# Weighted sums over 32 keys for two query blocks at once, in a fused sparse-attention and feed-forward kernel on one core

## The chip, the cores and the metric

The kernel runs on one core of a Trainium2 chip. The core has a matrix engine (TensorE, "PE" in the profile, with its weight loads shown apart as "PEld"), a vector engine (VectorE, "DVE"), a scalar engine (ScalarE, "ACT"), GpSimd ("POOL") and SyncE ("SP"), whose queue issues nearly all transfers here. Each engine works through its own list of instructions in order and waits on semaphores for the others. The metric is the device time of one execution in microseconds (us); less is better. Before the change it is 864.33 us, the median of 3 runs (864.06 to 865.29).

## The reference

Eight batches of eight heads, 576 positions, head size 64: four heads attend to a local band, four to a strided pattern; then a feed-forward layer over all 4608 tokens with a softplus between its two matrix products.

```python
rel = pos[:, None] - pos[None, :]
mask_local = (rel >= 0) & (rel < stride)                       # stride = 32
mask_strided = (rel >= 0) & (pos[None, :] % stride == pos[:, None] % stride)
scores = np.where(masks, q @ k.T / sqrt(64), -1e9)             # local for heads 0-3, strided for 4-7
attn = softmax(scores)                                         # with 1e-9 added to the sum
x = (attn @ v) laid out as (batch * position, head * 64)       # 4608 x 512
h = x @ w_in                                                   # 512 -> 2048
g = np.maximum(h, 0.0) + np.log1p(np.exp(-np.abs(h)))
out = g @ w_out                                                # 2048 -> 512
```

## The kernel before

**Pairs and chunks.** Heads are worked off in pairs, four pairs a batch, 32 pairs in all, numbered n = 0 to 31 in the order of work. The strided heads' positions are sorted by class on the host, so that for both kinds a block of 32 queries needs only its own block of 32 keys and the block ahead of it: 64 keys. A pair has 18 such query blocks; they are laid out as 9 "chunks" (x = 0 to 8) times two "places" (place 0: the first nine blocks of a head, place 1: the last nine). From the third batch on (n = 8 and up) this is the layout of `head_scores`, `add_mask`, `turn` and `late_sums`, which the change touches; the first eight pairs use other routines.

**One pair, from n = 8 on.** All of its matrix work is in fp32, and each matmul of the program runs as two passes on TensorE, each with a weight load: the trace counts two MATMUL and two LDWEIGHTS for each.

- `head_scores` (L406 to L428, all its matmuls at L422, task S): for each chunk, place and head a matmul with 64 rows of contraction (the head's dimensions), 32 queries as the weights and 64 keys as the moving operand: 36 matmuls. A tile of the array is set by the rows that a matmul reads (64 for each head) and by the partitions that it writes (32 for each query block). Chunks 0 to 5 ("part 0") go to the PSUM bank `ps`, chunks 6 to 8 ("part 1") to the right part of the bank `po`. In part 1 `place_of` (L402) swaps the two heads' partitions: head 0 is written where head 1 stands in part 0, and the other way round.
- Softmax on DVE and ACT: mask added out of PSUM (L481), maxima, subtraction, exponential, sums, division (L486 to L525).
- `turn` (L546 to L557, tasks P.0, P.1 and P): the probabilities, 128 partitions by 9 chunks by 64 keys, are transposed in squares of 32 on DVE into `turned`: one transpose of the whole tile, 128x576 (L550), and then four of 32x288 (two at L555, two at L557), which put the two 32-key halves of one head's block below each other, so that one matmul can contract 64 keys.
- `late_sums` (L559 to L574, task V, or inside the next pair's S): for each chunk, place and head one matmul with 64 rows (keys), 64 columns of weights (the values of one head) and 32 moving columns (queries): 36 matmuls, each complete in itself. Place 0 writes the bank `po`, place 1 the bank `pv`.
- `load_v` (L314 to L329) puts the values into `v_late` twice, once for each of the two query blocks that use a block of keys: one transfer of 32 rows and two of 64 rows in pieces of 512 bytes (both heads' 64 values of a key).
- ACT and DVE copy the result out of PSUM into the two halves of x (L691, L689).

**The rest** is the feed-forward layer: `hidden` (L774) and `output` (L843) with 128x512 matmuls, and for the last four of the nine column blocks of 512 tokens a scheme with fewer products (L946). Softplus and splitting of the operands is on ACT and DVE. The pairs n = 8 to 31 are slipped in between these matmuls: S of pair n and the weighted sums of pair n-1 as one block, every third step, and two of the 24 (n = 27 and 31) on their own.

**Order of the work.** The first tenth of a kernel run follows a list of names written out by hand (`FIRST`). After that `Plan` decides: each task has an urgency, an engine, an estimated cost and the tasks it comes after; `Plan` places the tasks in order of urgency at the first gap of their engine and then emits all of them in order of their planned start. So a cost or a dependency that changes can move instructions of other tasks on DVE, ACT and SP.

Of the kernel before, what the change touches and what calls it, by code (L numbers as in the profile page):

```python
# [18 lines left out]
P = 128  # L19
# [57 lines left out]
class Plan:  # L77
# [8 lines left out]
    def add(self, name, urgency, engine, cost, fn, after=(), late=0.0):  # L86
        self.tasks[name] = (urgency, len(self.tasks), engine, cost, fn, after, late)
# [29 lines left out]
def attention_softplus_ffn(  # L117
# [9 lines left out]
    nc = tc.nc  # L127
    B, NPAIR, _, _, S = qk.shape
    D = P // 2
# [6 lines left out]
    NCHK = NTILE * 3 // 2  # L136
# [30 lines left out]
    homes = [home(k, n, f"home_{k}") for k, n in enumerate(HOMES)]  # L167
# [41 lines left out]
    ]  # L209
    mask_late = homes[0][:, 3 * S : 3 * S + NCHK * 32].bitcast(BF16)  # L210
    v_late = homes[0][:, : 2 * S].rearrange("p (x d) -> p x d", d=2 * D)
    turned = homes[1][:, 2 * S : 3 * S].rearrange("p (c x l) -> p c x l", c=2, l=32)
    qT = homes[0][:, 2 * S : 3 * S]
    kT = [homes[2][:, i * (PAD + S) : (i + 1) * (PAD + S)] for i in range(2)]
    v_in = homes[1][:, 2 * S : 2 * S + 2 * NTILE * D]
# [21 lines left out]
    taken = []  # L237
    phs, us, ghs, gls, lent = {}, {}, {}, {}, {}
    HALF = NFC // 2
    SPILLED = (NCHUNK - 3,)  # L240
    PLAIN = [(NCHUNK - 3, HALF - 1), (NCHUNK - 3, NFC - 1)]
    ROWS = [list(range(NFC)) for _ in range(NCHUNK)]
# [28 lines left out]
    def prob_of(n):  # L271
        if n < NPAIR:
            chunks = prob_early[n][:, PAD:].rearrange("p (a c) -> p a c", c=3 * PAD)
            return chunks[:, :, :64]
        return prob[n % 2]

    raws = {}

    def load_q(n):

        b, pair = order[n]
        if n < NPAIR:
            t = w_pool.tile([P, 2 * DM], F32, tag=f"wo{12+n}", name=f"raw_q{n}")
            raws[n] = t[:, :S]
        else:
            raws[n] = prob[n % 2].rearrange("p a c -> p (a c)")
        nc.sync.dma_start(raws[n], qk[b, pair, :, 0])
# [25 lines left out]

    def load_v(n):  # L314
        b, pair = order[n]
        if n >= 2 * NPAIR:
            if n == 2 * NPAIR:
                nc.gpsimd.memset(v_late[:32, 0], 0.0)
            src = v[b, pair]
            nc.sync.dma_start(v_late[32:64, 0], src[:32])  # L320
            for place in range(2):
                lo = 1 - place
                keys = src[32 * (NCHK * place + lo - 1) :]
                keys = bass.AP(
                    tensor=keys.tensor,
                    offset=keys.offset,
                    ap=[[2 * D, 64], [32 * 2 * D, NCHK - lo], [1, 2 * D]],
                )
                nc.sync.dma_start(v_late[64 * place : 64 * place + 64, lo:], keys)  # L329
            return  # L330
        if n < NPAIR:

            t = room[n]
        else:
            t = v_in
        t = t[:, : 2 * NTILE * D].rearrange("p (a c) -> p a c", c=2 * D)
        src = v[b, pair]
        nc.sync.dma_start(t[PAD:P, 0], src[0:TILE])
        src = src[TILE - PAD : 2 * TILE]
        src = bass.AP(  # L340
            tensor=src.tensor,
            offset=src.offset,
            ap=[src.ap[0], [TILE * 2 * D, NTILE - 1], src.ap[1]],
        )
        nc.sync.dma_start(t[:, 1:NTILE], src)
        vs[n] = t.rearrange("p a (h d) -> p a h d", d=D)
# [52 lines left out]
        if n == 0:  # L399
            add(False)  # L400

    def place_of(part, h):  # L402

        return 1 - h if part == 1 else h

    def head_scores(n):  # L406

        taken.append(n)
        pss[n, 0] = ps_s.tile([P, 512], F32, tag="ps", name=f"ps_{n}")
        shared[n] = ps_o.tile([P, 512], F32, tag="po", name=f"po_{n}")  # L410
        pss[n, 1] = shared[n][:, S // 2 :]
        for x in range(6):
            for chunk in (x, x + 3) if x > 2 else (x,):
                part = chunk // 6
                for place in range(2):
                    a, i = block_at(chunk, place) if n < 2 * NPAIR else (3 * place, chunk)
                    c = TILE * a + 32 * i
                    for h in range(2):
                        to = 64 * place + 32 * place_of(part, h)
                        head = slice(64 * h, 64 * h + 64)  # L420
                        at = 64 * (chunk - SPLIT[part][0])
                        nc.tensor.matmul(  # L422
                            pss[n, part][to : to + 32, at : at + 64],
                            lhsT=qT[head, c : c + 32],
                            rhs=k_of(n)[head, c : c + 64],
                            start=True,
                            stop=True,
                        )  # L428
# [116 lines left out]

    def turn(n, step):  # L546

        src = prob_of(n).rearrange("p x (c l) -> p c x l", l=32)
        if step == 0:
            nc.vector.transpose(turned, src)  # L550
            return
        for place in range(2):
            lower, upper = (slice(at, at + 32) for at in (64 * place, 64 * place + 32))
            if step == 1:
                nc.vector.transpose(turned[upper, 0], src[lower, 1])  # L555
            else:
                nc.vector.transpose(turned[lower, 1], src[upper, 0])  # L557

    def late_sums(n, joint):  # L559

        if joint:
            to = [shared[n + 1], ps_h.tile([P, 512], F32, tag="ph", name=f"pv_{n}_1")]
        else:
            taken.append(n)
            to = [
                ps_o.tile([P, 512], F32, tag="po", name=f"pv_{n}_0"),
                ps_s.tile([P, 512], F32, tag="ps", name=f"pv_{n}_1"),
            ]
        pos[n, 0], pos[n, 1] = to
        for x in range(NCHK):  # L570
            for place in range(2):
                rows = slice(64 * place, 64 * place + 64)
                for h in range(2):
                    nc.tensor.matmul(  # L574
                        to[place][64 * h : 64 * h + 64, 32 * x : 32 * x + 32],
                        lhsT=v_late[rows, x, D * h : D * h + D],
                        rhs=turned[rows, place_of(x // 6, h), x],
                        start=True,
                        stop=True,
                    )  # L580
# [130 lines left out]
    part = {}  # L711
# [474 lines left out]
    add = plan.add  # L1186
# [18 lines left out]
    for i in range(begin, len(steps)):  # L1205
        c, f = steps[i]
        w, x = CH[c] / 384, when[i]
        after = [f"F{i-1}", f"u{i-2}", f"G{c}.{f}"] + lows_of(c)
# [3 lines left out]
        after = [f"F{i}", f"Us{i-2}" if f"Us{i-2}" in plan.tasks else f"l{i-2}"]  # L1212
# [4 lines left out]
        else:  # L1217
            after = [f"u{i}", f"O{i-3}"]
            add(f"h{i}", x + 4.1, "ACT", 0.65, lambda c=c, f=f: g_high(c, f, nc.scalar), after)
            after = [f"h{i}", f"O{i-3}"]  # L1220
            fn = lambda c=c, f=f: g_low(c, f, nc.vector)
# [4 lines left out]
        c, f = steps[k]  # L1226
        w = CH[c] / 384
        x = when[i] + 2.1 * w
# [5 lines left out]
        for t in range(nt):  # L1234
            name = f"O{k}" if t == nt - 1 else f"O{k}.{t}"
# [22 lines left out]
    def scores_of(n, x, y, name, e, cost, after, also=None):  # L1258

        z = x - 11.0  # L1260
        if n > 2 * NPAIR:
            add(f"Q{n}", z, "ACT", 1.4, lambda n=n: lay_out_q(n), [f"q{n}", f"S{n-1}"])

        def work():
            head_scores(n)
            if also is not None:
                sums_of(also)

        add(name, x, e, cost, work, after)
        for j in range(2):  # L1270
            fn = lambda j=j: add_mask(n, j)
            add(f"Y{n}{j}", y + j, "DVE", 0.47, fn, [f"S{n}", f"P{n-2}"])
        after = [f"Y{n}0", f"Y{n}1"]
        for j, (letter, e, cost, fn) in enumerate(
            (
                ("x", "DVE", 0.75, row_maxima),
                ("s", "DVE", 0.75, row_subtract),
                ("E", "ACT", 0.7, row_exp),
                ("z", "DVE", 0.75, row_sums),
                ("g", "DVE", 0.16, lambda n: guard(n, nc.vector)),  # L1280
                ("R", "DVE", 0.2, reciprocals),
                ("M", "DVE", 0.75, lambda n: normalize(n, nc.vector)),
            )
        ):
            add(f"{letter}{n}", y + 1.5 + j, e, cost, lambda fn=fn: fn(n), after)
            after = [f"{letter}{n}"]
        for j, (name, step, cost) in enumerate(
            ((f"P{n}.0", 0, 0.8), (f"P{n}.1", 1, 0.95), (f"P{n}", 2, 0.95))
        ):
            fn = lambda step=step: turn(n, step)  # L1290
            add(name, y + 8.5 + 0.9 * j, "DVE", cost, fn, after)
            after = [name]
        if n + 2 < len(order):
            add(f"k{n+2}", x + 5, "SP", 0.8, lambda: load_k(n + 2), [f"S{n}"], 2.0)
            add(f"q{n+2}", x + 18, "SP", 0.8, lambda: load_q(n + 2), [f"P{n}"], 2.0)
# [432 lines left out]
```

## Time and profile before

| | |
|---|---|
| Time, median of 3 runs | 864.33 us (864.06 to 865.29) |
| Profiled execution | 865.32 us, of which 863.5 us from its first to its last instruction (the span) |
| Busy: PE / PE weight loads | 853.9 us (99%) / 703.3 us |
| Busy: DVE / ACT / POOL | 584.3 us (68%) / 494.2 us (57%) / 66.4 us (8%) |
| DMA | 124.49 MB, mean 144 GB/s |

"Busy" is the time in which an engine had at least one instruction in flight; matmuls overlap in the pipeline, so PE at 99% does not say that it works at its peak. The views used below are: the page's parts; the groups by line with shapes kept apart, in which "64*32 64x64" means 64 rows of the array and 32 columns of weights used, and an operand of 64 partitions by 64 elements; the list of who waited for whom; the stretches ("windows") with each engine's busy time and number of instructions; and the timeline, in which each row has start, length, engine, line, operation, and how many instructions in a row were merged (the length then runs from the start of the first to the end of the last).

### The profile page before, as it was taken

To read this page: it belongs to the slowest core of one execution; us is meant where nothing else is said; L and a number is where in the kernel's file an instruction comes from. 1 tells how busy PE (TensorE), PEld (TensorE's weight loads), DVE (VectorE), ACT (ScalarE), POOL (GpSimd) and SP (SyncE) were. 2 spreads that over 40 slices of the span, in tenths; PEclk is the share of its full clock that TensorE was granted. 3 is DMA by queue.
4 is the path that set the end of the run, shared out by engine and by line. 5 is a ranking of instruction groups with operands and counts; after the bars stand their busy time and mean duration, and the time that the engine had idled before them with its cause. 6 is when DMAs were issued, how large, how long until landed. Compare 5 with 4: busy or idle time off the path is not lost.

```text
span 863.5 us, 18656 instructions
## 1 busy us (share of the span) xinstructions
PE 853.9 (99%) x7688; PEld 703.3 (81%) x7688; DVE 584.3 (68%) x1106; ACT 494.2 (57%) x913; POOL 66.4 (8%) x89
## 2 busy tenths in 40 slices
PE   7999999999999999999999999999999999999998
PEld 5787888888888888888888888788888888888886
DVE  7899977677686668776668866666687645656500
ACT  6998755665555555646555655766664355566400
POOL 6345550000000000000000000000000000000000
PEclk9999999999999999999999999999999999999999
DMA  9894215556422554326424543655546144333100
GB/s 325 286 354 152 58 47 195 184 161 217 137 84 90 171 149 130 104 80 200 130 76 149 155 125 118 198 177 187 174 148 209 50 158 135 109 123 122 45 29 24
DMA packets 85332, 124.49 MB, mean 144 GB/s; under 512 B 7296, under 2 KB 52480, under 8 KB 85248
## 3 DMA queue, kind: packets, MB, share of 16 engines
q1 hardware_dynamic: 84960, 122.99, 43.8%
q8 instruction: 60, 0.98, 0.5%
q10 hardware_dynamic: 288, 0.33, 0.1%
q14 instruction: 24, 0.20, 0.1%
HBM read 92.88 MB, written 30.41 MB: 143 GB/s over the span
## 4 chain that ended last, share of the span: by engine, by line
PE 93%; DMA 2%; DVE 2%; ACT 1%; issue 1%; POOL 0%; SPq 0%; ACTq 0%; POOLq 0%
PE py L843 43%; PE ph L774 24%; PE bank_a L946 10%; PE bank_c L946 5%; PE po L574 2%; PE bank_b L946 2%; DMA ro<-in_moe_w_out_dram 2%; PE ps L422 2%; PE py_last L843 1%; PE po L422 1%; PE pv L574 1%; PE pv L640 1%; PE pt L610 1%; DVE home L536 1%; DMA raw_q<-in_qk_dram 0%
## 5 line engine op out<-in xcount | busy, mean ns | idle before, releaser
L843 PE MATMUL py<-w_o,gh 128*128 128x512 f32 x1024 | 318.3, 392 | 0.0
L843 PEld LDWEIGHTS py<-w_o,gh 128*128 128x128 f32 x1024 | 190.4, 188 | 39.5
L774 PE MATMUL ph<-x_h,w_i 128*128 128x512 f32 x656 | 202.7, 390 | 0.5 <-DVE u L798 0.5
L843 PE MATMUL py<-w_o,gl 128*128 128x512 f32 x512 | 199.2, 389 | 0.0
L774 PEld LDWEIGHTS ph<-x_h,w_i 128*128 128x128 f32 x656 | 122.5, 188 | 26.7 <-POOL home L525 0.9
L774 PE MATMUL ph<-x_l,w_i 128*128 128x512 f32 x328 | 127.6, 389 | 0.0
L843 PEld LDWEIGHTS py<-w_o,gl 128*128 128x128 f32 x512 | 96.1, 188 | 20.2
L290 ACT CAST gh<-u 128x512 fp32r<-128x512 f32 x89 | 55.1, 621 | 96.4 <-DVE u L798 74.5
L786 ACT ACTIVATE u<-ph 128x512 f32<-128x512 f32 x84 | 50.2, 599 | 94.8 <-PE ph L774 92.2
L828 DVE TENSOR_TENSOR gl<-u,gh 128x512 fp32r<-128x512 f32 x117 | 80.8, 691 | 25.0 <-ACT gh L290 21.9
L789 ACT ACTIVATE u<-u 128x512 f32<-128x512 f32 x144 | 90.9, 633 | 3.8
L791 ACT ACTIVATE u<-u 128x512 f32<-128x512 f32 x144 | 90.8, 631 | 3.7
L798 DVE SCALAR_TENSOR_TENSOR u<-ph,u 128x512 f32<-128x512 f32 x84 | 57.7, 687 | 37.3 <-ACT u L791 36.6
L774 PEld LDWEIGHTS ph<-x_l,w_i 128*128 128x128 f32 x328 | 61.6, 188 | 13.0
L786 ACT ACTIVATE u<-kept 128x512 f32<-128x512 f32 x45 | 28.5, 633 | 42.4 <-DVE kept L1042 26.0
L290 DVE COPY o<-py 128x512 f32<-128x512 f32 (+1 forms) x15 | 10.0, 670 | 47.0 <-PE py L843 46.8
L481 DVE TENSOR_TENSOR home<-ps,home 128x384 f32<-128x384 f32 x28 | 15.5, 555 | 36.4 <-PE ps L422 34.9
L1042 DVE TENSOR_TENSOR kept<-bank_c,kept 128x512 f32<-128x512 f32 x15 | 10.4, 692 | 36.5 <-PE bank_c L946 35.2
L290 ACT COPY home<-home 128x576 f32<-128x576 f32 x26 | 33.5, 1290 | 1.6 <-DMA home<-in_qk_dram 1.6
L290 ACT COPY o<-py 128x512 f32<-128x512 f32 (+1 forms) x21 | 11.5, 575 | 38.1 <-PE py L843 27.3
L1037 ACT COPY kept<-bank_a 128x512 f32<-128x512 f32 x30 | 17.7, 589 | 25.5 <-PE bank_a L946 24.5
L422 PEld LDWEIGHTS ps<-home,home 64*32 64x32 f32 x1344 | 23.3, 106 | 9.9 <-issue 8.1
(205 smaller groups left out, 1299.5 us busy)
## 6 DMA issues: line engine op xcount, KB each, us to landing
home<-in_qk_dram SPq DMA_DIRECT2D x56, 288.0 KB, 3.5
ws<-far SPq DMA_DIRECT2D x30, 512.0 KB, 3.3
out_dram<-o SPq DMA_DIRECT2D x35, 256.0 KB, 2.3
ri<-in_moe_w_in_dram SPq DMA_DIRECT2D x16, 512.0 KB, 7.3
ro<-in_moe_w_out_dram SPq DMA_DIRECT2D x16, 512.0 KB, 8.3
far_w<-w_i SPq DMA_DIRECT2D x16, 512.0 KB, 4.5
w_i<-far_w SPq DMA_DIRECT2D x16, 512.0 KB, 3.4
near<-far_w SPq DMA_DIRECT2D x15, 512.0 KB, 3.3
```

The source lines that it names most:

```text
L290: (engine.copy if engine is nc.scalar else engine.tensor_copy)(dst, src)
L422: nc.tensor.matmul(pss[n, part][to : to + 32, at : at + 64], lhsT=qT[head, c : c + 32], rhs=k_of(n)[head, c : c + 64], start=True, stop=True,)
L574: nc.tensor.matmul(to[place][64 * h : 64 * h + 64, 32 * x : 32 * x + 32], lhsT=v_late[rows, x, D * h : D * h + D], rhs=turned[rows, place_ ...
L774: nc.tensor.matmul(ph, lhsT=w_i(c, f)[:, half, cc * P : (cc + 1) * P], rhs=x_at(x, cc, c), start=(i == 0), stop=(i == 3 * NCC - 1),)
L786: nc.scalar.activation(us[c, f], phs[c, f], AF.Abs)
L789: nc.scalar.activation(u, u, AF.Exp, scale=-1.0)
L791: nc.scalar.activation(u, u, AF.Ln, bias=1.0)
L798: nc.vector.scalar_tensor_tensor(to, in0=ph, scalar=0.0, in1=u, op0=ALU.max, op1=ALU.add)
L828: engine.tensor_tensor(g, us.pop((c, f)), ghs[c, f].bitcast(F32), op=ALU.subtract)
L843: nc.tensor.matmul(y_of(c, t), lhsT=g[:, sl], rhs=w32["o", f][:, half], start=(f == ROWS[c][0] and n == 0), stop=(f == ROWS[c][-1] and n = ...
L946: nc.tensor.matmul(bank, lhsT=w_left(p, A, f, half, i), rhs=x_right(p, A, part, i), start=p in "125" and n == 0, stop=n == 5, skip_group_c ...
L1037: nc.scalar.copy(kept(A, s), bank_of(p, A, f))
```

## The change

From n = 8 on (`is_whole`), a weighted sum takes one block of 32 keys at a time and serves both query blocks that see it. The values are stored once per block of keys, with one head in each quarter of the partitions (`v_whole`). The probabilities are transposed by the one 128x576 instruction alone, so that the two halves of a query block's 64 keys stand next to each other in columns instead of below each other in partitions; a matmul then has 32 rows, 64 columns of weights and 64 moving columns (32 queries that see these keys as their second half, 32 that see them as their first half). Each block of queries is added up in PSUM by two matmuls that follow each other. At the ends of the row of chunks only 32 moving columns are left. The scores' part 1 is no longer swapped, since head and partition quarter must now go together. `load_v` has four transfers of 32 rows in pieces of 256 bytes. The plan has one task for the transposes in place of three.

```diff
-    turned = homes[1][:, 2 * S : 3 * S].rearrange("p (c x l) -> p c x l", c=2, l=32)
+    turned_all = homes[1][:, 2 * S : 3 * S]
+    turned = turned_all.rearrange("p (c x l) -> p c x l", c=2, l=32)
+    v_whole = homes[0][:, : (NCHK + 1) * D].rearrange("p (x d) -> p x d", d=D)
...
+    WHOLE = range(2 * NPAIR, 8 * NPAIR)
...
+    def is_whole(n):
+
+        return n in WHOLE
...
     def load_v(n):
         b, pair = order[n]
+        if is_whole(n):
+            src = v[b, pair].rearrange("(x l) (h d) -> l x h d", l=32, h=2)
+            for quarter in range(4):
+                place, h = divmod(quarter, 2)
+                lo = 1 - place
+                rows = slice(32 * quarter, 32 * quarter + 32)
+                keys = src[:, NCHK * place + lo - 1 : NCHK * place + NCHK, h]
+                nc.sync.dma_start(v_whole[rows, lo:], keys)
+            return
...
-    def place_of(part, h):
+    def place_of(part, h, n=0):
 
-        return 1 - h if part == 1 else h
+        return 1 - h if part == 1 and not is_whole(n) else h
...
     def turn(n, step):
 
+        if is_whole(n):
+            blocks = prob_of(n).rearrange("p x (c l) -> p (x c) l", l=32)
+            nc.vector.transpose(turned_all.rearrange("p (x l) -> p x l", l=32), blocks)
+            return
...
         pos[n, 0], pos[n, 1] = to
+        if is_whole(n):
+            for x in range(NCHK + 1):
+                for quarter in range(4):
+                    place, h = divmod(quarter, 2)
+                    if x + place == 0:
+                        continue
+                    lo, hi = max(64 * x - 32, 0), min(64 * x + 32, 64 * NCHK)
+                    at = max(32 * x - 32, 0)
+                    rows = slice(32 * quarter, 32 * quarter + 32)
+                    nc.tensor.matmul(
+                        to[place][64 * h : 64 * h + 64, at : at + hi - lo],
+                        lhsT=v_whole[rows, x],
+                        rhs=turned_all[rows, lo:hi],
+                        start=x + place == 1,
+                        stop=x == NCHK,
+                        skip_group_check=True,
+                    )
+            return
...
-        for j, (name, step, cost) in enumerate(
-            ((f"P{n}.0", 0, 0.8), (f"P{n}.1", 1, 0.95), (f"P{n}", 2, 0.95))
-        ):
+        turns = ((f"P{n}.0", 0, 0.8), (f"P{n}.1", 1, 0.95), (f"P{n}", 2, 0.95))
+        if is_whole(n):
+            turns = ((f"P{n}", 0, 0.8),)
+        for j, (name, step, cost) in enumerate(turns):
             fn = lambda step=step: turn(n, step)
-            add(name, y + 8.5 + 0.9 * j, "DVE", cost, fn, after)
+            add(name, y + 8.5 + 0.9 * j, "DVE", cost, fn, after + [f"V{n-1}"] * (j == 0))
             after = [name]
```

How the instructions now stand. On PE, the block of scores of pair 9 and weighted sums of pair 8, from the last feed-forward matmul before it to the first after it; `ps` and `po` are the banks of the scores, `po` and `pv` those of the sums, and each row counts matmuls of the program. Before (the nine pairs of rows of the sums are cut to the first and the last; all are alike):

```order
L774 MATMUL ph_5_1992<-x_l_594,w_i_807 128x512
L422 MATMUL ps_2012<-home_96,home_94 32x64 x16
L422 MATMUL po_2013<-home_96,home_94 32x64 x4
L422 MATMUL ps_2012<-home_96,home_94 32x64 x4
L422 MATMUL po_2013<-home_96,home_94 32x64 x4
L422 MATMUL ps_2012<-home_96,home_94 32x64 x4
L422 MATMUL po_2013<-home_96,home_94 32x64 x4
L574 MATMUL po_2013<-home_95,home_94 64x32 x2
L574 MATMUL pv_1_2050<-home_95,home_94 64x32 x2
```

```order
L574 MATMUL pv_1_2050<-home_95,home_94 64x32 x2
L843 MATMUL py_106<-w_o_948,gh_3_1963 128x512 x2
```

And now, again with the first rows and the last rows of the sums:

```order
L438 MATMUL po_2018<-home_96,home_94 32x64 x4
L599 MATMUL pv_1_2055<-home_95,home_94 64x32 x2
L599 MATMUL po_2018<-home_95,home_94 64x64 x2
L599 MATMUL pv_1_2055<-home_95,home_94 64x64 x2
```

```order
L599 MATMUL pv_1_2055<-home_95,home_94 64x64 x2
L599 MATMUL po_2018<-home_95,home_94 64x32 x2
L599 MATMUL pv_1_2055<-home_95,home_94 64x32 x2
L881 MATMUL py_106<-w_o_948,gh_3_1964 128x512 x2
```

The sums have 38 matmuls where there were 36: 18 for place 0 and 20 for place 1, 34 of them with 64 moving columns and 4 with 32. The rows of the scores and all feed-forward rows on PE stand as they stood.

On DVE, the end of the softmax of one pair in the middle of the kernel, before and now (`st` and `home_95` hold the pair's sums and probabilities, `u_4` is the feed-forward's):

```order
L521 RECIPROCAL st_4285<-st_4285 128x9
L525 TENSOR_TENSOR home_95<-home_95,st_4285 128x576
L550 STREAM_TRANSPOSE home_95<-home_95 128x576
L555 STREAM_TRANSPOSE home_95<-home_95 32x288 x2
L557 STREAM_TRANSPOSE home_95<-home_95 32x288 x2
L798 SCALAR_TENSOR_TENSOR u_4_4332<-ph_4_4299,u_4_4332 128x512
```

```order
L537 RECIPROCAL st_4273<-st_4273 128x9
L541 TENSOR_TENSOR home_95<-home_95,st_4273 128x576
L566 STREAM_TRANSPOSE home_95<-home_95 128x576
L836 SCALAR_TENSOR_TENSOR u_4_4321<-ph_4_4288,u_4_4321 128x512
L1045 TENSOR_TENSOR ww_0_4255<-ww_0_4253,ww_0_4255 128x256
```

The four small transposes are gone and what stood behind them moves up.

On SP, one stretch of the queue before and now (`in_qk_dram` are the loads of queries and keys, `far_w` stores of a weight tile):

```order
L752 DMA far_w_2861<-w_i_1242 128x1024
L287 DMA home_95<-in_qk_dram 128x576
L752 DMA far_w_2967<-w_i_1569 128x1024
L312 DMA home_96<-in_qk_dram 128x576
L859 DMA out_dram<-o_0_2978 128x512
L320 DMA home_94<-in_v_dram 32x128
L329 DMA home_94<-in_v_dram 64x8x128
L329 DMA home_94<-in_v_dram 64x9x128
```

```order
L294 DMA home_95<-in_qk_dram 128x576
L790 DMA far_w_2860<-w_i_1242 128x1024
L790 DMA far_w_2961<-w_i_1569 128x1024
L319 DMA home_96<-in_qk_dram 128x576
L897 DMA out_dram<-o_0_2972 128x512
L330 DMA home_94<-in_v_dram 32x9x64 x2
L330 DMA home_94<-in_v_dram 32x10x64 x2
```

The load of the next queries, which comes after the pair's transposes, stands earlier by one to two places here and in several other stretches, ahead of stores and loads of weight tiles; and the values come by four transfers where there were three.

More of the change, by code (lines that the diff above doesn't have):

```diff
@@ L315, in load_v @@
         b, pair = order[n]
+        if is_whole(n):
[7 more added lines that the diff above has]
+            return
         if n >= 2 * NPAIR:
-            if n == 2 * NPAIR:
+            if n - 1 in WHOLE or n == 2 * NPAIR:
                 nc.gpsimd.memset(v_late[:32, 0], 0.0)
@@ L418, in head_scores @@
                     for h in range(2):
-                        to = 64 * place + 32 * place_of(part, h)
+                        to = 64 * place + 32 * place_of(part, h, n)
                         head = slice(64 * h, 64 * h + 64)
```

## The prediction

> **What bounds the kernel now.** I read the page's first, second and fourth parts, then the list of who waited for whom with TensorE's own rows, then the windows, and last the timeline of one block of scores and sums.
>
> ```profile
> PE 853.9 (99%) x7688; PEld 703.3 (81%) x7688; DVE 584.3 (68%) x1106; ACT 494.2 (57%) x913; POOL 66.4 (8%) x89
> PEclk9999999999999999999999999999999999999999
> PE 93%; DMA 2%; DVE 2%; ACT 1%; issue 1%; POOL 0%; SPq 0%; ACTq 0%; POOLq 0%
> ```
>
> TensorE is in flight nearly all the time, its granted clock in the top tenth throughout, and the chain that ended last runs through it. Since "busy" can hide a stall, its waits are the better witness:
>
> ```profile
> PE ph L774 <- DVE u L798: 0.5, 1, 0.5
> PEld ps L422 <- issue: 8.1, 23, 0.4
> PEld bank_a L946 <- DVE kept L1042: 0.5, 1, 0.5
> PEld pv L574 <- PE py L843: 0.4, 1, 0.4
> 150.00:508.00 358.00, 358.00 (x4183) 296.00 (x4182) 258.27 (x494) 203.38 (x351) 0.00 (x0) 1.00 0.45 138
> 560.00:700.00 140.00, 140.00 (x1085) 115.78 (x1084) 91.52 (x161) 76.43 (x130) 0.00 (x0) 1.00 0.47 151
> ```
>
> The first rows give total, times and longest: where the scores and sums stand TensorE waits for another engine about once, for half a microsecond. The 8.1 us at "issue" are 23 times the same 0.35 us ahead of a block of scores, when the array changes from 128x128 to small tiles; nobody releases it. In the windows (length, then busy time of PE, PEld, DVE, ACT, POOL) PE fills the stretches in which nearly all changed pairs lie. So what decides is how long TensorE's own stream of instructions gets, and nothing that another engine saves.
>
> **How long a block of small matmuls takes.** One block, PE alone:
>
> ```profile
> 412.81 0.39 PE L774 MATMUL ph<-x_l,w_i 128*128 128x512 f32 x1
> 413.13 0.26 PE L422 MATMUL ps<-home,home 64*32 64x64 f32 x4
> 413.13 0.32 PE L422 MATMUL ps<-home,home 64*32 64x64 f32 x8
> 413.13 0.37 PE L422 MATMUL ps<-home,home 64*32 64x64 f32 x12
> 413.13 0.43 PE L422 MATMUL ps<-home,home 64*32 64x64 f32 x16
> 413.13 0.48 PE L422 MATMUL ps<-home,home 64*32 64x64 f32 x20
> 413.40 0.24 PE L422 MATMUL po<-home,home 64*32 64x64 f32 x1
> 413.43 0.23 PE L422 MATMUL ps<-home,home 64*32 64x64 f32 x3
> 413.92 0.27 PE L422 MATMUL po<-home,home 64*32 64x64 f32 x4
> 414.12 0.25 PE L574 MATMUL po<-home,home 64*64 64x32 f32 x2
> 414.20 0.23 PE L574 MATMUL po<-home,home 64*64 64x32 f32 x2
> 415.13 0.23 PE L574 MATMUL po<-home,home 64*64 64x32 f32 x2
> 415.30 0.73 PE L843 MATMUL py<-w_o,gh 128*128 128x512 f32 x2
> 23.16 0.64 PE L610 MATMUL pt<-room,early_l 128*64 128x64 f32 x16
> L610 PE MATMUL pt<-room,early_l 128*64 128x64 f32 x144 | 6.3, 223 | 3.2 <-issue 2.8 <-POOL early_l L525 0.4
> ```
>
> The rows from 413.13 are one run of matmuls, asked for with a later end each time. They come in groups of four, one pass on each of four tiles of the array, and a further group adds (0.48 - 0.26) / 4 = 0.055 us. The sums at L574 come in groups of four too (two on `po`, two on `pv`); from the second of their 18 groups at 414.20 to the last at 415.13 are 16 steps of 0.058 us. The last two rows are of an early transpose by matmul on two tiles, 64 columns of weights and 64 moving columns: eight groups of two, each 0.22 us long (mean 223 ns), so (0.64 - 0.22) / 7 = about 0.059 us a step. So three shapes have nearly one step: 32 weight columns and 64 moving (0.055), 64 and 32 (0.058), 64 and 64 (0.059). A tile seems to take about 0.055 us to stream 64 columns and 0.058 us to load 64 columns of weights, the two overlap, and the longer sets the step. The 128 rows of the last shape against 64 of the other two make no difference.
>
> **The sums.** They go from 36 matmuls (18 steps on each tile) to 38, of which the two tiles of place 1 have ten each, 20 steps. The shape is 64 weight columns by 64 moving, over 32 rows. Nearest is L610 with both column counts; its step equals that of today's sums within the rows' rounding, so I take 0.058: two steps more, **+0.116 us a block**. Bounds: if 20 steps went at the stream's 0.055, +0.05; at 0.059, +0.13; the far ends are two of the rivals. That half of the arithmetic done in each added column is new costs nothing in this reading: today's 32 moving columns hide behind the weight load.
>
> **The scores.** Their rows do not change, yet they get slower. With the heads swapped, part 1 (`po`) goes to the other four of the eight tiles, and TensorE runs it beside part 0: the first `po` matmul starts at 413.40 with 20 passes of `ps` begun, though 16 matmuls, 32 passes, of `ps` stand ahead of it in the program. From 413.13 to 414.19 (413.92 + 0.27) all takes 1.06 us. Unswapped, all 18 groups queue on the same four tiles: 0.26 + 17 x 0.055 = 1.195 us, **+0.14 us** with the step's rounding. Bounds: 0, if the order of tiles should not matter, and +0.15 at a step of 0.056.
>
> The page "TensorE: Matmul & The Clock Gate" of the Trainium skill says under "The mechanism" (small matmuls on tiles) that matmuls start and end strictly in program order. By that rule unswapping could cost nothing. The row at 413.40 speaks against it, and only the sums' term would stay if it held.
>
> The gaps around the blocks (413.92 to 414.12, 415.13 to 415.30) are changes of tiling, two of which a pair keeps, now to a shape of 32 rows that the trace does not have. I take them as they are; a second such change of 0.1 us each would add at most 24 x 0.2 = 4.8 us.
>
> **DVE.** It loses the four small transposes of each pair:
>
> ```profile
> L555 DVE STREAM_TRANSPOSE home<-home 32x288 f32<-32x288 f32 x48 | 22.5, 470 | 1.1
> L557 DVE STREAM_TRANSPOSE home<-home 32x288 f32<-32x288 f32 x48 | 22.5, 470 | 0.7
> L550 DVE STREAM_TRANSPOSE home<-home 128x576 f32<-128x576 f32 x24 | 18.7, 779 | 0.8
> 423.54 0.95 DVE L557 STREAM_TRANSPOSE home<-home 32x288 f32<-32x288 f32 x2
> 432.83 0.25 PE L574 MATMUL po<-home,home 64*64 64x32 f32 x2
> ```
>
> That is 45.0 us of DVE, 1.9 us a pair; the large transpose stays. I put its worth at nothing: the last transpose ends at 424.49 and its sums start at 432.83, 8.3 us later. Ahead of the pair's own softmax nothing on PE waits for DVE. If all of TensorE's mid-kernel waits for DVE vanished, that would be 1 us (two rows of 0.5 above).
>
> **Transfers.** Four of 32 rows in 256-byte pieces replace three of up to 64 rows in 512-byte pieces.
>
> ```profile
> 414.67 0.38 SPq L320 DMA_DIRECT2D home<-in_v_dram  x1
> 415.40 2.21 SPq L329 DMA_DIRECT2D home<-in_v_dram  x2
> home<-in_v_dram SPq DMA_DIRECT2D x24, 288.0 KB, 4.1
> home<-in_v_dram SPq DMA_DIRECT2D x24, 256.0 KB, 4.2
> home<-in_v_dram SPq DMA_DIRECT2D x24, 16.0 KB, 3.5
> 413.23 0.32 SPq L757 DMA_DIRECT2D w_i<-far_w  x1
> w_i<-far_w SPq DMA_DIRECT2D x16, 512.0 KB, 3.4
> 423.59 0.61 PE L774 MATMUL ph<-x_h,w_i 128*128 128x512 f32 x2
> ```
>
> Today the values are issued by 417.61 and land about 4.2 us later, 11 us ahead of the sums at 432.83; the bytes fall (19 blocks of 32 keys and two heads' 64 values are 304 KB, against 560 in the three rows). Even double the time stays hidden; past that cover, each microsecond late costs one. SP's queue is also passed in another order: loads of queries, which wait for a pair's transposes, now stand ahead of some weight tiles. A weight tile issued at 413.23 is used at 423.59, some 6.6 us after it lands; the transposes that the load waits for end 1.9 us earlier than today. Nothing.
>
> **Sum.** Scores +0.14, sums +0.116, so +0.256 us a block. Sums: 936 + 792 passes are 24 blocks of 72; scores from pair 8 on are 24 too. 24 x 0.256 = **+6.1 us**. On the profiled execution: a span of 863.5 to 869.6, its time 865.32 to 871.4; it ran 1.0 us above the median of the runs. On the median: 864.33 + 6.1 = **870.5 us**, slower by 0.7%.
>
> ```profile
> L574 PE MATMUL pv<-home,home 64*64 64x32 f32 x936 | 29.7, 220 | 0.0
> L574 PE MATMUL po<-home,home 64*64 64x32 f32 x792 | 27.2, 220 | 0.0
> ```
>
> **Rivals.**
> *Only the sums' term (10%).* Scores keep 1.06 us: +2.8 us, 867.1. For it: the matmuls are the same; against it: the row at 413.40. With the sums at 0.055 a step as well, it ends at +1.3 us, too little to measure; that end gets 5 points of its own.
> *Fewer rows, faster matmuls (5%).* The other side: a tile of 32 rows loads and streams in half the time of 64. Then 20 steps of 0.029 make 0.58 us against 18 x 0.058 = 1.04; with the scores' +0.14 that is -0.32 a block, -7.7 us, **856.6**. It would decide from a step below (1.04 - 0.14) / 20 = 0.045 us. Against it: 64 and 128 rows have the same step.
> *Row tiles of one bank take turns (8%).* Heads 0 and 1 of a place now read different rows and write one bank (`po` or `pv`); today's sums of one bank share their rows. If each such pair alternated, a step is 2 x 0.055: 20 x 0.11 = 2.2 us against 1.04, with the scores +1.3 a block, **+31 us, 895**. Against it: in today's scores the two heads read different rows, all four tiles write `ps`, and a group still takes 0.055.
> "TensorEngine Tiling (Array Packing)" of the Trainium skill, "Gotcha 1: PSUM Pressure", states that rule, that different row tiles cannot access one PSUM bank at the same time; the scores' groups of four do not show it.
> *A transfer or the new tiling costs more (2%)*: up to +11 us, 875.
>
> **Chances.** Forecast 70%, the others as given. A measurement here cannot tell less than 0.2% (1.7 us) from no change. Faster 5%, the case of fewer rows; same 5%, the low end of the first rival; slower 90%, all others. The range runs from just under the sums' term alone, 866.8, to both terms at their upper bounds (24 x 0.28 = 6.7) with most of the tiling's extra 4.8 us: 875.0.
>
> **What would show it.** In the changed profile: the scores' block 1.19 to 1.21 us long with no `po` pass until 32 of `ps` have begun; the sums' groups 0.058 us apart, 20 of them; a block of scores and sums about 0.26 us longer; DVE near 539 us busy; TensorE still without waits. Wrong if the sums' step is not near 0.058, if the scores keep their length, or if PE shows waits for DVE or a DMA between 150 and 700 us.

## The result, and the profile after

| | before | after |
|---|---|---|
| Time, median of 4 runs each | 864.57 us (864.06 to 865.29) | 871.58 us (870.43 to 873.57) |
| Profiled execution (span) | 865.32 us (863.5) | 871.65 us (869.9) |

The changed kernel is slower: the ratio is 1.0079, 95% interval 1.0062 to 1.0096, which is 6.8 us (5.4 to 8.3). The forecast was 870.5 us; the two profiled executions are 6.3 us apart, the forecast's sum was 6.1.

The page of the changed kernel, busy times and the chain that ended last:

```profile
PE 860.5 (99%) x7784; PEld 709.6 (82%) x7784; DVE 538.9 (62%) x1010; ACT 494.1 (57%) x913; POOL 65.8 (8%) x88
PE 92%; ACT 3%; DVE 3%; issue 1%; DMA 0%; POOL 0%; ACTq 0%; POOLq 0%
```

PE is busy 6.6 us longer, DVE 45.4 us less, and the chain still runs through PE. Does PE wait for anything new? The list of who waited for whom (total, times, longest), PE's rows of the middle of the kernel:

```profile
PEld ps L438 <- issue: 8.8, 25, 0.4
PE ph L812 <- DVE u L836: 0.5, 1, 0.5
PEld pv L599 <- PE py L881: 0.4, 1, 0.4
```

And the same two windows as before (length, then busy time of PE, PEld, DVE, ACT, POOL):

```profile
150.00:508.00 358.00, 358.00 (x4171) 296.81 (x4170) 221.25 (x416) 201.60 (x347) 0.00 (x0) 1.00 0.40 124
560.00:700.00 140.00, 140.00 (x1097) 115.89 (x1096) 85.61 (x147) 77.74 (x132) 0.00 (x0) 1.00 0.47 147
```

No new wait: PE fills both windows as it did. So the time is in the length of its own stream. One block of scores (L438) and sums (L599) in the timeline of PE, the counterpart of the block from 412.81 to 415.30 before:

```profile
416.50 0.39 PE L812 MATMUL ph<-x_l,w_i 128*128 128x512 f32 x1
416.82 0.65 PE L438 MATMUL ps<-home,home 64*32 64x64 f32 x32
417.30 0.29 PE L438 MATMUL po<-home,home 64*32 64x64 f32 x8
...
417.74 0.29 PE L438 MATMUL po<-home,home 64*32 64x64 f32 x8
417.96 0.24 PE L599 MATMUL pv<-home,home 32*64 32x32 f32 x2
...
418.19 0.22 PE L599 MATMUL pv<-home,home 32*64 32x64 f32 x2
...
418.94 0.22 PE L599 MATMUL pv<-home,home 32*64 32x64 f32 x2
...
419.25 0.73 PE L881 MATMUL py<-w_o,gh 128*128 128x512 f32 x2
```

Three things are to be seen. All 32 passes of `ps` now run before the first of `po`, where before `po` began after 20. The sums' groups on `pv` go in 13 steps from 418.19 to 418.94, 0.058 us each. And the block, from the last big matmul ahead of it to the first behind it, has grown from 2.49 to 2.74 us. At the trace's full resolution the scores take 0.993 us from first to last start (0.843 before), the sums 1.136 (1.032), and the gaps around them are as they were within 3 ns: 0.252 us a block, 6.05 us in 24.

The line view of the two kernels shows the same from a distance (count, shortest, median and longest in ns, then the first and the last start in us). Before:

```profile
L422 PE MATMUL ps<-home,home x1344: 216/216/240, 32.7 to 644.5; 64*32 64x64 f32 x192
L574 PE MATMUL pv<-home,home x936: 219/219/240, 152.1 to 671.6; 64*64 64x32 f32 x188
```

After:

```profile
L438 PE MATMUL ps<-home,home x1344: 216/216/240, 32.7 to 650.4; 64*32 64x64 f32 x192
L599 PE MATMUL pv<-home,home x1032: 190/217/265, 152.3 to 677.8; 32*64 32x64 f32 x139, 32*64 32x32 f32 x33
```

The scores start at 32.7 in both; from there to the last sums it is 638.9 us before and 645.1 after, +6.3 at the trace's full resolution. What lies ahead and behind adds 0.1.

Now the cover of the transposes, in the timeline of DVE and of PE after the change:

```profile
425.69 0.78 DVE L566 STREAM_TRANSPOSE home<-home 128x576 f32<-128x576 f32 x1
436.94 0.24 PE L599 MATMUL pv<-home,home 32*64 32x32 f32 x2
```

The one transpose of this pair ends at 426.47 and its sums start at 436.94: 10.5 us of slack where there were 8.3. The transfers of the values, in the page's list of DMA issues (the last number is the time to landing):

```profile
home<-in_v_dram SPq DMA_DIRECT2D x48, 80.0 KB, 2.4
home<-in_v_dram SPq DMA_DIRECT2D x48, 72.0 KB, 2.9
```

They land in 2.4 and 2.9 us against 3.5 to 4.2.

### The profile page after: what moved, and what is told of

Its sections match the earlier page's. It is cut to its first block, busy times and chain, and to the rows that moved or that the text cites. A ratio compares the mean times of both kernels' runs of the same rounds, so it can differ in the third digit from the quotient of the medians.

```text
span 869.9 us, 18802 instructions
## 1 busy us (share of the span) xinstructions
PE 860.5 (99%) x7784; PEld 709.6 (82%) x7784; DVE 538.9 (62%) x1010; ACT 494.1 (57%) x913; POOL 65.8 (8%) x88
## 4 chain that ended last, share of the span: by engine, by line
PE 92%; ACT 3%; DVE 3%; issue 1%; DMA 0%; POOL 0%; ACTq 0%; POOLq 0%
PE py L881 42%; PE ph L812 23%; PE bank_a L984 9%; PE bank_c L984 5%; PE pv L599 3%; PE ps L438 2%; PE bank_b L984 2%; PE py_last L881 1%; PE po L438 1%; PE po L599 1%; ACT home L518 1%; PE pt L648 1%; DVE home L552 1%; PE pv L678 0%; DMA raw_q<-in_qk_dram 0%
## 5 line engine op out<-in xcount | busy, mean ns | idle before, releaser
L599 PE MATMUL pv<-home,home 32*64 32x64 f32 (+1 forms) x1032 | 32.5, 218 | 0.0
```

The lines of the kernel that those rows point to most:

```text
L599: nc.tensor.matmul(to[place][64 * h : 64 * h + 64, at : at + hi - lo], lhsT=v_whole[rows, x], rhs=turned_all[rows, lo:hi], start=x + place ...
```

## The experiments

The theory: TensorE's own stream sets the time; the scores lose 0.150 us a block since all their groups queue on four tiles, the sums 0.104 since two tiles have 20 steps where they had 18; nothing else counts. Each run was timed beside runs of the kernel before on its own chip: their median is 864.60 us of 20 runs for the two halves and the first two orders, 864.42 of 19 for the others.

**Scores alone.** The kernel before, with part 1 unswapped in the changed pairs; the sums and transposes stay.

```diff
-    def place_of(part, h):
-        return 1 - h if part == 1 else h
+    def place_of(part, h, n=0):
+        return 1 - h if part == 1 and n < 2 * NPAIR else h
```

> The kernel before with one thing undone: from pair 8 on the two heads are no longer swapped in part 1 of the scores; sums, transposes and loads stay as before. Theory (each tile of the array has its own queue, and the swap lets part 1 run beside part 0 on the other four tiles): the block of scores grows from 1.06 us to about 1.21 us, as in the changed kernel; 24 x 0.15 = +3.6 us, 868.2. Rival (matmuls run strictly in program order, the scores' growth in the changed kernel has another cause, such as the new tiling of the sums behind them): scores stay at 1.06, time stays at 864.6.

Measured: 869.35 us, ratio 1.0066 (1.0044 to 1.0088), +5.7 us (3.8 to 7.6); the medians are 4.8 apart. The block in the timeline of PE:

```profile
415.12 0.39 PE L774 MATMUL ph<-x_l,w_i 128*128 128x512 f32 x1
415.44 0.65 PE L422 MATMUL ps<-home,home 64*32 64x64 f32 x32
415.91 0.29 PE L422 MATMUL po<-home,home 64*32 64x64 f32 x8
...
416.36 0.29 PE L422 MATMUL po<-home,home 64*32 64x64 f32 x8
416.58 0.25 PE L574 MATMUL po<-home,home 64*64 64x32 f32 x2
...
417.76 0.74 PE L843 MATMUL py<-w_o,gh 128*128 128x512 f32 x2
...
420.65 0.61 PE L774 MATMUL ph<-x_h,w_i 128*128 128x512 f32 x2
```

The same 36 matmuls, only written elsewhere, take 0.993 us in place of 0.843: the scores' term is shown, in the very pattern of the changed kernel (32 `ps`, then `po`). The 24 blocks add 3.62 us; from the first scores to the last sums the trace adds 4.6. The missing 1.0 us lies behind the blocks, as its last two rows show: from the first big matmul behind the block to the thirteenth it is 2.89 us (417.76 to 420.65). Before it was 2.85, from 415.30 to this row of PE's timeline:

```profile
418.15 0.61 PE L774 MATMUL ph<-x_h,w_i 128*128 128x512 f32 x2
```

Of those twelve intervals, eight or nine are 3 to 10 ns longer, with the same operands; nearly every stretch behind a block is 0.04 us longer in this way. In the changed kernel it is 0.01 us (419.25 to 422.11 for the same thirteen). Why is open.

**Sums alone.** The changed kernel, with the scores' swap kept.

```diff
-                        to = 64 * place + 32 * place_of(part, h, n)
+                        to = 64 * place + 32 * place_of(part, h)
```

> The changed kernel with the heads swapped in part 1 of the scores again, as before; the sums don't know of it, so in chunks 6 to 8 each head's probabilities are weighted with the other head's values (that part of the output is wrong, the work is the same). Theory (two terms that add up): scores back to 1.06 us, sums stay at 1.14 between first and last start against 1.03, 24 x 0.104 = +2.5 us against before, 867.1; with the other run of this call the two terms give the whole change. Rival (the new tiling or the new order of transfers and vector work costs something by itself): more than 868.

Measured: 867.61 us, ratio 1.0037 (1.0022 to 1.0052), +3.2 us (1.9 to 4.5); the medians are 3.0 apart. Its block, timeline of PE:

```profile
413.79 0.39 PE L812 MATMUL ph<-x_l,w_i 128*128 128x512 f32 x1
414.11 0.48 PE L438 MATMUL ps<-home,home 64*32 64x64 f32 x20
414.38 0.24 PE L438 MATMUL po<-home,home 64*32 64x64 f32 x1
...
414.90 0.27 PE L438 MATMUL po<-home,home 64*32 64x64 f32 x4
415.10 0.24 PE L599 MATMUL pv<-home,home 32*64 32x32 f32 x2
...
416.38 0.72 PE L881 MATMUL py<-w_o,gh 128*128 128x512 f32 x2
```

The scores are back at 0.843 us, with `po` starting after 20 passes of `ps`; the sums keep 1.136, and the block takes 2.59 us. In the blocks the two halves of the loss add up to the whole: 3.62 + 2.44 = 6.06, against 6.05. The halves by their ratios, +5.7 and +3.2, add up to more than the 6.8 of the change, but their intervals reach down to 5.7 together. The run also says that a version of this change which could keep the swap would still be slower than before.

The Trainium skill, "TensorE: Matmul & The Clock Gate", section "The mechanism", has matmuls start and end strictly in program order. The row at 414.38 is against it: 32 passes of `ps` stand ahead of that `po` pass in the program, and 20 have begun. In the run before this one, where `po` needs the same four tiles as `ps`, the order is the program's.

**The transposes alone.** The kernel before, without its four small transposes.

```diff
         if step == 0:
             nc.vector.transpose(turned, src)
+        if step >= 0:
             return
```

> The kernel before without the four small transposes of each pair from pair 8 on (the sums then weight half of each head's probabilities from the wrong place, so that part of the output is wrong; all other work stays, and so does the plan of three tasks). Theory (TensorE waits for nothing that DVE does): DVE's busy time falls by 45 us to about 539, the time stays at 864.6, within 1 us. Rival (DVE's work is on the path somewhere, and the change won there what it lost on TensorE): faster by 2 us or more.

Measured: 864.48 us, ratio 1.0003 (0.9994 to 1.0013). The page's busy times:

```profile
PE 853.5 (99%) x7688; PEld 703.3 (82%) x7688; DVE 539.3 (63%) x1010; ACT 493.8 (57%) x913; POOL 66.1 (8%) x89
```

DVE is at 539.3 us, as in the changed kernel, and the time does not move: the 45 us are worth nothing here, which the interval bounds at 0.5 us of gain.

**What sets the sums' step.** The changed kernel with 32 moving columns in place of 64 in nearly all sums; the weights, the rows and the number of matmuls stay.

```diff
                     at = max(32 * x - 32, 0)
+                    if hi - lo == 64 and x + place > 1:
+                        lo, at = lo + 32, at + 32
```

> The changed kernel with 32 moving columns in nearly every matmul of the sums in place of 64 (each block of queries then gets one of its two blocks of keys; that half of the sum is left out). Theory (the load of 64 weight columns sets the step): the step stays at 0.057 to 0.058 us and the sums' 20 steps as long as in the changed kernel; the profiled span stays at 869.9 within 0.5. Rival (the stream of 64 columns sets it, the load of 32 rows is quicker than that of 64): the step falls to about 0.03 us, each block by 0.5 us, the span by 12 us.

One execution: 870.4 us, span 868.6. Timeline of PE, sums on `pv`:

```profile
416.97 0.22 PE L601 MATMUL pv<-home,home 32*64 32x32 f32 x2
...
417.73 0.23 PE L601 MATMUL pv<-home,home 32*64 32x32 f32 x2
...
418.00 0.73 PE L883 MATMUL py<-w_o,gh 128*128 128x512 f32 x2
```

Between the two rows are 13 steps again, 0.058 us each, and all blocks together last as long as in the changed kernel. Half the moving columns save nothing, so streaming does not set the step; the load of 64 weight columns is what stays the same. With more moving columns it does: an early routine, which no edit touches, has 96 of them to the same 64 weight columns. Timeline of PE in the run of the scores alone, six groups of two passes on two tiles:

```profile
60.15 0.67 PE L640 MATMUL pv<-home,home 128*64 128x96 f32 x12
```

Its step is 0.082 us at the trace's full resolution. So 64 moving columns are hidden behind 64 weight columns and 96 are not, which fits the longer of two times. That the shorter limit, 0.058, is the weight load itself is not shown: no run changes the weight columns alone. The span missed its expectation by 0.8 us, and by something else: the first scores start at 31.4 us in place of 32.7.

By the Trainium skill, "TensorE: Matmul & The Clock Gate", section "LDWEIGHTS (loading the stationary operand)", a weight load takes its time by columns and not by rows of contraction; 64 columns make 53 ns by its formula, an estimate. The traces agree on the rows (0.058 us with 64 rows before, 0.058 with 32 after), and their step is 5 ns longer than that figure.

**Does the order of the scores matter?** If tiles that stand idle are what the swap uses up, then another order of the chunks should do better still in the kernel before. Two orders, both with the swap; the loop also computes the scores of pairs 4 to 7, so 28 blocks are touched.

```diff
-        for x in range(6):
-            for chunk in (x, x + 3) if x > 2 else (x,):
+        for x in range(1):
+            for chunk in (0, 6, 1, 2, 7, 3, 4, 8, 5):
```

> The kernel before with the chunks of the scores in another order, 0 6 1 2 7 3 4 8 5 in place of 0 1 2 3 6 4 7 5 8; nothing else. Theory (queues per tile): part 1's tiles get work from the start, the block of scores shrinks from 1.06 us towards the 12 steps of part 0's tiles, 0.26 + 11 x 0.056 = 0.88 us at best; with half of that gain 28 x 0.09 = -2.5 us, 862, with all of it -5 us, 859.6. Rival (strict program order): no change, 864.6.

Measured: 863.02 us, ratio 0.9985 (0.9975 to 0.9994), 1.3 us faster. Timeline of PE:

```profile
409.88 0.26 PE L422 MATMUL ps<-home,home 64*32 64x64 f32 x4
409.90 0.26 PE L422 MATMUL po<-home,home 64*32 64x64 f32 x4
...
410.55 0.29 PE L422 MATMUL ps<-home,home 64*32 64x64 f32 x5
410.77 0.25 PE L574 MATMUL po<-home,home 64*64 64x32 f32 x2
411.96 0.74 PE L843 MATMUL py<-w_o,gh 128*128 128x512 f32 x2
...
414.85 0.62 PE L774 MATMUL ph<-x_h,w_i 128*128 128x512 f32 x2
```

Both banks' passes begin 0.02 us apart and mix to the end; the scores take 0.754 us, 0.09 less, 2.5 us in 28 blocks. About 1.1 us of it is given back by the trace, most of it where the first experiment lost it: from the first big matmul behind the block to the thirteenth it is 2.89 us (411.96 to 414.85) in place of 2.85.

The second order is 6, 0, 7, 1, 8, 2, 3, 4, 5, with part 1 as early as it can be.

```diff
+            for chunk in (6, 0, 7, 1, 8, 2, 3, 4, 5):
```

> The same with the order 6 0 7 1 8 2 3 4 5, part 1 first in each of three turns. Theory (queues per tile): between 859.6 and 862 again; whether earlier is better than evenly spread shows how far ahead TensorE takes matmuls out of the program. Rival (strict program order): no change, 864.6. A wait for the bank po, which is now asked for first, would show as idle time of PE ahead of the scores.

Measured: 864.84 us, ratio 0.9997 (0.9985 to 1.0009), no gain. Timeline of PE:

```profile
412.64 0.26 PE L422 MATMUL po<-home,home 64*32 64x64 f32 x4
412.67 0.26 PE L422 MATMUL ps<-home,home 64*32 64x64 f32 x4
...
413.10 0.60 PE L422 MATMUL ps<-home,home 64*32 64x64 f32 x28
413.63 0.25 PE L574 MATMUL po<-home,home 64*64 64x32 f32 x2
```

Part 1 is through by 413.10, and then 28 passes of `ps` have four tiles to themselves at 0.056 us a group while the other four are idle. The block is as long as before (0.843). What counts is that both sets of tiles have work until the end.

**The same order without the swap.** The changed kernel with the order 0, 6, 1, 2, 7, 3, 4, 8, 5 (the edit of above).

> The changed kernel with the chunks of the scores in the order 0 6 1 2 7 3 4 8 5, which shortened the block by 0.09 us in the kernel before. Theory (it is the other four tiles that shorten it): without the swap all chunks queue on the same four tiles, the block stays at 0.99 us from first to last start; only the scores of pairs 4 to 7, which are still swapped, get shorter, 4 x 0.09 = -0.4 us of span. Rival (the order by itself helps, by the two banks or otherwise): the block shortens by 0.09 here too, -2.5 us.

One execution: 870.18 us, span 868.4, its first scores at 31.3 us. Timeline of PE:

```profile
415.35 0.32 PE L438 MATMUL ps<-home,home 64*32 64x64 f32 x8
415.49 0.29 PE L438 MATMUL po<-home,home 64*32 64x64 f32 x8
415.60 0.40 PE L438 MATMUL ps<-home,home 64*32 64x64 f32 x16
...
416.27 0.29 PE L438 MATMUL ps<-home,home 64*32 64x64 f32 x8
```

The passes go strictly in the program's order and the scores keep 0.993 us in all changed pairs; the blocks as a whole are 0.37 us shorter, all of it in the four pairs that still swap. So it is neither the second bank nor the order by itself that lets the scores of the kernel before run faster, but the other four tiles.

**A still finer spread.** The kernel before, with half a chunk of part 1 after every chunk of part 0.

```diff
-            for chunk in (x, x + 3) if x > 2 else (x,):
+            for chunk, places in ((x, (0, 1)), (6 + x // 2, (x % 2,))):
...
-                for place in range(2):
+                for place in places:
```

> The kernel before with part 1 spread finer: after each chunk of part 0, one place of a chunk of part 1. Theory (queues per tile, part 1 runs beside part 0 as far as it comes early enough): the block of scores between the 0.754 us that the coarser spread gave from first to last start and the 0.66 of part 0's twelve steps alone; 28 x (0.843 - 0.70) = -4 us against before, 860.6. Rival (what limits it now is how fast matmuls are handed to the array, not their order): 0.75 again, 862.

Measured: 862.74 us, ratio 0.9979 (0.9966 to 0.9992), 1.8 us faster than before (0.7 to 2.9). With the coarser spread it is the version that beats both kernels; the two intervals overlap, so which is better is not told. The block of scores is 0.754 us again, by PE's timeline:

```profile
411.13 0.26 PE L422 MATMUL ps<-home,home 64*32 64x64 f32 x4
...
411.87 0.23 PE L422 MATMUL po<-home,home 64*32 64x64 f32 x2
412.03 0.25 PE L574 MATMUL po<-home,home 64*64 64x32 f32 x2
```

Twelve groups alone on one set of tiles take 0.66 us from first to last start (the first twelve groups of the changed kernel's 18). Neither spread gets there, and both end at the same 0.754, some 21 ns for each of the 36 matmuls of the program. A limit on handing matmuls to the array would do that; no run here takes it apart.

## Why the prediction was right, step by step

- **TensorE's own stream bounds, with no new wait**: right. PE has the same few waits after as before, and the 24 blocks, at 6.05 us, hold nearly all of the 6.3 us that the trace adds from the first scores to the last sums.
- **Scores, +0.14 us a block** for queueing on four tiles: right in kind, measured +0.150. It stood on a step of 0.055 read from rows of two decimals; its upper bound was 0.15 at 0.056, which is the step at the trace's full resolution. Scores alone and the same order without the swap show the mechanism: same matmuls, other tiles.
- **Sums, +0.116 us a block** for two steps more: the mechanism is right, the size 0.012 too large; measured +0.104. The step in the middle is 0.058 as forecast, but at the start and the end of a run of sums the steps are uneven, and the two added ones come to 0.052 each. The two errors nearly cancel, which is luck: 0.256 forecast, 0.252 measured. Two small sums of the forecast are off as well: (0.64 - 0.22) / 7 is 0.060 and not 0.059 (the starts in the trace give 0.058), and the bounds of the sums' term come to +0.06 and +0.14 in place of +0.05 and +0.13. Neither moves the forecast.
- **The weight load sets the sums' step, so 32 rows neither gain nor lose, and the doubled moving columns are free**: what follows from it is right. The step is 0.058 us with 64 and with 32 rows, and stays so with 32 moving columns. That it is the load of the weights that takes this time is argued from the shapes and not shown by itself.
- **Gaps of the new tiling as they are**: right within 3 ns. What lies behind the gap, the first big matmuls, was not in the sum; it came to 0.2 us over all blocks.
- **DVE's 45 us and the transfers worth nothing**: right for DVE, by the run without the small transposes. For the transfers only the trace speaks (quicker landing, no wait of PE for a DMA); none was changed by itself.
- **The rivals.** Only the sums' term (867.1): what it gives is measured, 867.61, in the kernel that keeps the swap, and the change goes beyond it. Fewer rows, faster matmuls (856.6): it needed a step below 0.045. Row tiles of one bank take turns (895): it needed a step of 0.11. A dearer tiling (875): the gaps did not change.

The median rose by 7.0 us, the trace by 6.3. The difference is within what runs of one kernel differ by, and the start alone can make as much: the first scores begin between 30.4 and 32.7 us over the ten traced kernels, one execution of each, and no edit touches the matmuls ahead of them.

## What to carry to other kernels

Where TensorE has no waits, cost a change by the queue of each tile of its array: count the groups that each tile must run in a row, and multiply by the step of the shape, which here did not go by the rows: 0.056 us for 32 weight columns and 64 moving ones, 0.058 for 64 weight columns with 32 or 64 moving ones, 0.082 with 96. A rewrite like this one, which halves the rows of the matmuls and fills idle moving columns, saves nothing if the busiest tile gets more weight loads, and work saved on an engine with microseconds of slack pays for none of it. When small matmuls can go to several sets of tiles, give every set work until the end of the block: an even mix gained 0.2%, where the same work with one set served first gained nothing.

## What the runs showed that was not expected

- The scores of the kernel before had 0.09 us a block left in them, by order alone. It stops at 0.754 us for 36 matmuls with either spread, above the 0.66 us of twelve groups per tile; what stops it is open.
- A block of small matmuls changes the big ones behind it. With the scores unswapped or evenly mixed in the kernel before, most of the first eleven intervals between 128x512 matmuls are 3 to 10 ns longer, 0.04 us a block, and about 1 us in the whole kernel; with the changed sums 0.01 to 0.02. The kernels differ in how many intervals pass before they settle at 0.227 us: five in the kernel before, seven in the changed one, ten with the changed sums alone, eleven with the scores alone. This ate about 1 of the 2.5 us that the better order gained, and its cause is open.
